# Batch 0 of an attention-and-FFN kernel: mask by a product, single PSUM banks, first weights issued behind the V casts

## The chip, the cores and the metric

The kernel runs on one core of a Trainium2 chip. The metric is the device time of one execution in microseconds (us), lower is better. The median of 7 runs of the kernel before is 380.16 us (379.72 to 381.32).

## The reference

Inputs are `q`, `k`, `v` of shape (8 batches, 8 heads, 576 rows, 64), `s` of shape (8, 8, 576), and the weights `w_gate`, `w_val` (512 x 1536) and `w_out` (1536 x 512), all float32. The attention has a bias that decays with the running sum of `s`, and a causal mask:

```
scores = q @ k.T / 8
cum    = cumsum(max(s, 0))
scores = where(col > row, -1e9, scores + min(-(cum[row] - cum[col]), 0))
attn   = softmax(scores);  x = (attn @ v), heads side by side: 4608 tokens x 512
g = x @ w_gate;  out = (g * sigmoid(g) * (x @ w_val)) @ w_out      # 4608 x 512, float32
```

## The kernel before

**Attention.** A *half batch* is four heads (0 to 3 of a batch, or 4 to 7); there are 16, numbered `hb`. K and Q come in by SyncE's DMA queue (`load_qk`), are cast to bf16 (`cast_half`, `cast_one`), transposed so that the 64 dimensions lie on partitions, and copied into the tile `KQ[hb % 2][r]`, where `r` picks the pair of heads within the half batch. For `hb` up to 4 TensorE does the transposing (`pe_transpose`, `pe_out`), later ones go through DRAM and a transposing DMA (`scratch`, `transposes`, `split`). Besides the 64 dimensions, four more rows of `KQ` hold the running sum of `s` and ones, so that the score product adds the bias by itself; `aug` brings them by small DMAs (`kq<-HL`).

Scores stand transposed: keys on partitions, queries along the free axis. Per head `score_piece` makes four chunks of 512, 512, 512 and 64 columns (`CHUNKS`); chunks 0 and 3 are the blocks on the diagonal, which alone need a mask. ScalarE takes the exponential (L388) into the tile `pt`, GpSimd sets the masked half of the diagonal blocks to zero (`affine_select`, L391 for 512 columns and L396 for 64). `av_piece` multiplies with V, which has a column of ones so that the row sums come along (L413); `av_out` divides on VectorE (L429, L430) into `ot`, two heads side by side. `x_pe` transposes a pair of heads on TensorE into `XT`, the FFN's input (four pairs make the 512 features); later batches do it by DMA (`xs<-ot`, `XT<-xs`).

**FFN.** It goes over nine tiles of 512 tokens (`tt`). Per tile `gate_value` makes 12 gate products (L626) and 12 value products (L641) of 128 x 512, each a sum over four 128-deep parts; ScalarE takes tanh (L631), VectorE multiplies (L633, L649). `down_plain` (tiles 0 and 1, L670) and `down_seven` (L711) multiply with `w_out`.

**Order.** Nothing is scheduled by a planner: each engine works through its instructions in the order in which the program writes them. Batch 0 is written out in `first_batch`. After it, tile `tt` of the FFN is interleaved with attention of batch `tt + 1`: `ffn_items` yields after each product, and `pump` advances `attn_items` up to a position in proportion. `hook` puts a few steps behind the first FFN items, `side` puts loads, casts and copies between the chunks of scores, and `later` holds the copies out of the transposing DMA (`split`, L284), which `do_later` releases one by one.

**PSUM.** There are 8 banks of 512 float32 columns. In batch 0 four of them form two double banks (`wide`), so that a head's scores take two exponentials, of 1024 and 576 columns; the other four serve all else. `second_psum` changes to eight single banks after batch 0. `take` gives the bank that was released first.

**Queues of batch 0.** SyncE's DMA queue has, in this order: `s`, K and Q of half batches 0 and 1, `aug(0)`, V of batch 0, K and Q of half batch 2, `aug(2)`, `aug(3)` (these wait until the scores that read the old rows are done), K and Q of half batch 3, V of batch 1, K and Q of half batches 4 and 5. GpSimd's DMA queue has `aug(1)` and the weights (`w_load`): they are read as float32 and land as bf16, in halves of 768 KB: `g` 0 and `v` 0 behind the scores of head 1, `g` 1 behind head 4, `v` 1 behind head 5, and both halves of `w_out` behind head 7. GpSimd also casts three of the five pieces of V(0), VectorE the other two. In the steady part GpSimd casts V(1) (L183), issues `aug(4)` (L197) and casts K and Q of half batch 4 (L256), in this order.

```
wq = {1: (("g", 0), ("v", 0)), 4: (("g", 1),), 5: (("v", 1),)}
tail = {
    6: ("a0", "a1"),
    7: ("a2", "a3", "a4", "x0", "a5", "x1", "a6", "a7", "x2", "w6", "x3", "w8"),
}
```

Here `a` is a head's values, `x` a pair's transpose and `w` a number of warming products (128-wide products on the identity, whose result nobody reads).

Of the kernel before, what the change touches and what calls it, by code (L numbers as in the profile page):

```python
# [19 lines left out]
def kernel(  # L20
# [86 lines left out]
    PTP = {0: first, "bufs": 8}  # L107

    with tc.manual_schedule():
# [3 lines left out]
        first_psum = ExitStack()  # L113
        psa = first_psum.enter_context(tc.tile_pool(name="psa", bufs=1, space=PSUM))
        bank = {}
        for i in range(2):
            bank["w", i] = psa.tile([128, 1024], FP32, name=f"wide{i}")
        for i in range(4):
            bank["s", i] = psa.tile([128, 512], FP32, name=f"one{i}")
        released = {key: i - 8 for i, key in enumerate(bank)}  # L120
# [3 lines left out]
        def take(kind="s"):  # L124
            b = min((x for x in bank if x[0] == kind), key=lambda x: released[x])
            assert released[b] < OPEN
            released[b] = OPEN
            return b
# [5 lines left out]
        def second_psum():  # L134
            assert all(x < OPEN for x in released.values())
            at_end = dict(released)
            first_psum.close()
            psb = ctx.enter_context(tc.tile_pool(name="psb", bufs=1, space=PSUM))
            bank.clear()
            released.clear()  # L140
            for i in range(8):
                bank["s", i] = psb.tile([128, 512], FP32, name=f"bank{i}")
                released["s", i] = at_end["w", i // 2] if i < 4 else at_end["s", i - 4]

# [6 lines left out]
        def load_one(hb, name, rs=(0, NR)):  # L151
            b, g = divmod(hb, 2)
            if rs[0] == 0:
                loaded[name, hb] = raw.tile([128, NR, J, D], FP32, tag="raw" + name, name="raw" + name)
            nc.sync.dma_start(
                loaded[name, hb][:, rs[0] : rs[1], :, :].rearrange("x r j d -> x r (j d)"),
                SRC[name][0][b, g * HB + 2 * rs[0] : g * HB + 2 * rs[1], :, :].rearrange(
                    "(r e) (p j) d -> (e p) r (j d)", e=2, j=J
                ),
            )  # L160
# [5 lines left out]
        def load_v(b, cs):  # L166
            if 0 in cs:
                loaded["v", b] = raw.tile([128, NCH, H, D], FP32, tag="rawv", bufs=1, name="rawv")
            t = loaded["v", b]
            for c in cs:  # L170
                n = 128 if c < 4 else TAIL
                nc.sync.dma_start(  # L172
                    t[0:n, c, :, :],
                    v[b, :, c * 128 : c * 128 + n, :].rearrange("h p d -> p h d"),
                )
# [10 lines left out]
        NEGS2 = -1.0058441162109375  # L186

# [29 lines left out]
        make_identity(nc, ident)  # L217

# [11 lines left out]
        init_vt(0)  # L230
        init_vt(1)
# [116 lines left out]
        scs = {}  # L348

        def score_piece(bh, ci):  # L350
            hb, hh = divmod(bh, HB)
            pair = bh < H
            if ci == 0:
                pts[bh] = PTP[0].tile(
                [128, PTW], BF16, tag="pt", bufs=PTP["bufs"], name="pt"
            )
# [3 lines left out]
            if pair:  # L360
                if ci % 2 == 0:
                    bs = take("w")
                    scs[bh] = bs
                else:
                    bs = scs[bh]
                base = (512, 0, 0, 512)[ci]
            else:
                bs = take()
                base = 0
            o = base  # L370
            n = sum(hi - lo for _, lo, hi in CHUNKS[ci])
            sc = view(bs, 1024 if pair else 512)
            for (tj, lo, hi) in CHUNKS[ci]:
                w = hi - lo
                nc.tensor.matmul(  # L375
                    sc[:, o : o + w],
                    T[:, 1, e * S + 128 * tj : e * S + 128 * (tj + 1)],
                    T[:, 0, e * S + lo : e * S + hi],
                    start=True,
                    stop=True,  # L380
                )
                o += w
            if not pair or ci % 2 == 1:
                if pair:
                    c0, W = ((576, 1024), (0, 576))[ci // 2]
                else:
                    c0, W = CHUNK_PT[ci], n
                nc.scalar.activation(pt[:, c0 : c0 + W], sc[:, 0:W], AF.Exp, scale=0.125)  # L388
                give(bs)
            if ci == (1 if pair else 0):  # L390
# [90 lines left out]
        def side(h, step, ci):  # L481
# [7 lines left out]
            if NPE <= hb < NHB:  # L489
# [5 lines left out]
                first = 1 if hb < NPE + 2 else 0  # L495
# [31 lines left out]

        def prep_one(hb, i):
# [3 lines left out]
            for r in range(2):  # L532
                pe_out(hb, nm, g, r, nc.scalar if nm == "k" else nc.vector)

        PREP_AT = {
            2: {(0, 3): 0, (1, 3): 1, (2, 1): 2, (2, 3): 3},
# [81 lines left out]

        def gate_value(tt, hps, sus):
            xt = XT[:, :, (tt % 3) * TT : (tt % 3 + 1) * TT]  # L620
            for ft in range(NFT):
                j, f0 = divmod(ft * 128, WCH)
                gbs = take()
                pg = view(gbs, TT)
                for c in range(4):
                    nc.tensor.matmul(  # L626
                        pg, WG[j][:, c, f0 : f0 + 128], xt[:, c, :],
                        start=(c == 0), stop=(c == 3),
                    )
# [8 lines left out]
                vbs = take()  # L638
                pv = view(vbs, TT)
                for c in range(4):  # L640
                    nc.tensor.matmul(  # L641
                        pv, WV[j][:, c, f0 : f0 + 128], xt[:, c, :],
                        start=(c == 0), stop=(c == 3),
                    )
# [209 lines left out]

        cast_half(0, "k", 0, nc.scalar)
# [4 lines left out]
        for nm in ("k", "q"):  # L860
            for g in range(2):
                pe_transpose_half(0, nm, g, 0)
        pe_out(0, "k", 0, 0, nc.scalar)
        pe_out(0, "k", 1, 0, nc.scalar)
        pe_out(0, "q", 0, 0, nc.vector)
        pe_out(0, "q", 1, 0, nc.vector)
# [3 lines left out]
        for nm, eng in (("k", nc.scalar), ("q", nc.vector)):  # L870
            for g in range(2):
                pe_transpose_half(0, nm, g, 1)
                pe_out(0, nm, g, 1, eng)
        cast_one(1, "k", nc.vector)
        cast_one(1, "q", nc.vector)

        def keep_warm(n):
            bs = take()
            for _ in range(n):
                nc.tensor.matmul(  # L880
                    view(bs, 128), ident, ident, start=True, stop=True
                )
            give(bs)

        def first_batch():
            wq = {1: (("g", 0), ("v", 0)), 4: (("g", 1),), 5: (("v", 1),)}
            tail = {
                6: ("a0", "a1"),
                7: ("a2", "a3", "a4", "x0", "a5", "x1", "a6", "a7", "x2", "w6", "x3", "w8"),
            }  # L890
            for h in range(H):
                for ci in range(4):
                    score_piece(h, ci)
                for w in wq.get(h, ()):
                    w_load(*w)
                if h == 1:
                    order = [(nm, g) for g in range(2) for nm in ("k", "q")]
                    for nm, g in order:
                        pe_transpose(1, nm, g)
                    for r in range(2):  # L900
                        for nm, g in order:
                            pe_out(1, nm, g, r, nc.vector)
                    for c in range(3, 5):
                        cast_v(0, c, nc.vector)
                if h == 2:
                    for c in range(3):
                        cast_v(0, c, nc.gpsimd)
                if h == 3:
                    aug(2, SP4)
                if h == 7:  # L910
                    aug(3, SP4)
                    load_qk(3)
                    load_v(1, range(5))
                    load_qk(4)
                    cast_one(2, "k", nc.gpsimd)
                    cast_one(2, "q", nc.gpsimd)
                    load_qk(5)
                    w_load("o", 0)
                    w_load("o", 1)
                for what in tail.get(h, ()):  # L920
                    i = int(what[1:])
                    if what[0] == "a":
                        av_piece(i, range(NCH))
                        av_out(i)
                    elif what[0] == "x":
                        x_pe(i, nc.scalar)
                    else:
                        keep_warm(i)

        first_batch()  # L930
        second_psum()
# [6 lines left out]
        def pump(upto):  # L938
# [13 lines left out]
            4: [lambda: prep_one(2, 3)],  # L952
            6: [lambda: cast_one(3, "k", nc.gpsimd), lambda: cast_one(3, "q", nc.gpsimd)],
        }
        for tt in range(NTT):
# [11 lines left out]
            for i, cost in enumerate(ffn_items(tt)):  # L967
# [3 lines left out]
                if i >= 2 * NFT or i % 4 == 1:  # L971
                    do_later(1)
                for f in hook.pop(n, ()):
                    f()
# [32 lines left out]
```

The softmax here doesn't subtract the row's maximum and nothing guards it: scores larger than these inputs give would overflow.

## Time and profile before

| | |
|---|---|
| median of 7 runs | 380.16 us (379.72 to 381.32) |
| the profiled execution | 380.84 us, its span 379.0 us |
| TensorE matmul busy (PE) | 360.3 us (95%) |
| weight loads (PEld), VectorE (DVE), ScalarE (ACT), GpSimd (POOL) | 229.3, 290.6, 242.4, 206.7 us |
| granted TensorE clock | 1.0 in the page |
| DMA | 64.22 MB, mean 169 GB/s; q1 (SyncE) 46.15 MB, q0 (GpSimd) 17.53 MB |
| first score product, first gate product | 11.29 us, 31.27 us |

A line of the profile's groups names line, engine, operation and tile. "Busy" of PE counts a matmul from its start to a modelled end, 379 ns for 512 columns, though the next one may start 216 ns after it; so a gap of TensorE's work is read from the starts as well as from the listed waits. `SPq` is SyncE's queue: the engine stands at a DMA issue until the queue takes it. Times in a timeline are us from the span's start.

### The profile page before, as it was taken

Reading aid. Unit: us, or ns where it says so; the run is one execution under the profiler, and the core shown is the slowest. Engines: PE = TensorE matmul, PEld = TensorE weight load, DVE = VectorE, ACT = ScalarE, POOL = GpSimd, SP = SyncE. Lnnn points to the kernel's source line nnn. Section 1 sums busy time; section 2 is a strip of 40 time slices with the busy share of each in tenths; the row PEclk is TensorE's granted clock in tenths of the full one; section 3 lists DMA queues with packets and bytes.
Section 4 is the critical chain, followed back from the end, with each engine's and each line's share of the span. In section 5 each row is a group of like instructions: output and inputs, shape, how many; then the busy total and the mean of one; then the engine's idle time right before and its main releaser. Section 6 shows DMA issues by size and latency. Waiting matters only on the chain.

```text
span 379.0 us, 8635 instructions
## 1 busy us (share of the span) xinstructions
PE 360.3 (95%) x3207; PEld 229.3 (61%) x3246; DVE 290.6 (77%) x577; ACT 242.4 (64%) x459; POOL 206.7 (55%) x326
## 2 busy tenths in 40 slices
PE   3789999999999999999999999999999999999996
PEld 3565555655555555965586558755775575466465
DVE  7676776647895899869976999589958876985984
ACT  7686787687986777568767875697365523323321
POOL 7693338455365645595558656775675526224320
PEclk9999999999999999999999999999999999999999
DMA  7899999999478997499769865998233023001103
GB/s 245 186 255 262 199 190 310 319 279 193 159 168 272 214 292 188 120 233 291 159 205 266 219 164 162 226 197 159 48 74 118 20 32 128 0 2 66 45 2 111
DMA packets 100729, 64.22 MB, mean 169 GB/s; under 512 B 81888, under 2 KB 85824, under 8 KB 100688
## 3 DMA queue, kind: packets, MB, share of 16 engines
q1 hardware_dynamic: 91248, 46.15, 49.9%
q0 software_dynamic: 9440, 17.53, 18.7%
q8 instruction: 25, 0.41, 0.5%
q14 instruction: 16, 0.13, 0.1%
HBM read 37.90 MB, written 19.86 MB: 152 GB/s over the span
## 4 chain that ended last, share of the span: by engine, by line
PE 80%; DMA 6%; DVE 4%; SPq 4%; ACT 2%; issue 1%; POOL 1%; DVEq 0%
PE bank L641 20%; PE bank L626 20%; PE bank L711 17%; PE bank L375 8%; PE bank L413 6%; PE bank L670 5%; SPq L172 4%; DMA rawv<-in_v_dram 4%; PE wide L375 2%; ACT pt L388 2%; DMA xs<-ot 1%; DMA kq<-HL 1%; DMA s_sb<-in_s_dram 1%; DVE ht L649 1%; DVE pp L633 1%
## 5 line engine op out<-in xcount | busy, mean ns | idle before, releaser
L388 ACT ACTIVATE pt<-bank 128x512 bf16<-128x512 f32 x224 | 106.8, 506 | 26.1 <-PE bank L375 17.0
L626 PE MATMUL bank<-XT,wg 128*128 128x512 bf16 x420 | 109.7, 379 | 1.2 <-DVE pp L633 0.2
L641 PE MATMUL bank<-XT,wv 128*128 128x512 bf16 x411 | 109.3, 379 | 1.4 <-DMA wv<-in_moe_w_val_dram 0.3
L631 ACT ACTIVATE th<-bank 128x512 bf16<-128x512 f32 x108 | 64.7, 599 | 59.5 <-PE bank L626 55.4
L633 DVE SCALAR_TENSOR_TENSOR pp<-th,bank 128x512 bf16<-128x512 bf16 x108 | 73.7, 682 | 25.9 <-ACT th L631 25.3
L649 DVE SCALAR_TENSOR_TENSOR ht<-pp,bank 128x512 bf16<-128x512 bf16 x108 | 74.1, 686 | 10.5 <-PE bank L641 0.3
L658 POOL TENSOR_TENSOR ht<-ht 128x512 bf16<-128x512 bf16 x35 | 40.5, 1156 | 52.9 <-DVE su L656 52.8
L375 PE MATMUL bank<-kq 128*128 128x128 bf16 (+4 forms) x504 | 67.5, 240 | 0.1
L375 PEld LDWEIGHTS <-kq 128*128 128x128 bf16 x576 | 46.6, 99 | 33.0 <-issue 4.7
L641 PEld LDWEIGHTS <-wv 128*128 128x128 bf16 x432 | 38.3, 98 | 35.8 <-DMA wv<-in_moe_w_val_dram 0.5
L626 PEld LDWEIGHTS <-wg 128*128 128x128 bf16 x432 | 38.4, 98 | 35.3 <-issue 1.3
L391 POOL TENSOR_SCALAR_AFFINE_SELECT pt<-pt 128x512 bf16<-128x512 bf16 x64 | 41.3, 646 | 30.5 <-ACT pt L388 30.0
L413 PEld LDWEIGHTS <-pt 128*128 128x128 bf16 x960 | 41.2, 98 | 17.0 <-issue 1.1
L413 PE MATMUL bank<-vt,pt 128*128 128x65 bf16 x840 | 42.2, 194 | 0.8 <-DVE ot L430 0.5
L447 POOL DMA_DIRECT2D xs<-ot x24 | 21.8, 907 | 28.1 <-DVE ot L430 28.1
L711 PEld LDWEIGHTS <-ht 128*128 128x128 bf16 x336 | 31.2, 98 | 4.3
L197 POOL DMA_DIRECT2D kq<-HL x52 | 32.1, 620 | 0.1
L430 DVE TENSOR_TENSOR ot<-bank,rc 128x320 bf16<-128x320 f32 x56 | 27.5, 491 | 1.9
L396 POOL TENSOR_SCALAR_AFFINE_SELECT pt<-pt 128x64 bf16<-128x64 bf16 x64 | 17.5, 274 | 18.1 <-ACT pt L388 18.0
L711 PEld LDWEIGHTS <-su 128*128 128x128 bf16 x252 | 23.6, 98 | 3.3
L670 PE MATMUL bank<-wo,ht 128*128 128x512 bf16 x90 | 24.2, 379 | 0.3
L776 POOL TENSOR_TENSOR ysb<-ysb 128x512 f32<-128x512 f32 x12 | 15.2, 1270 | 15.3 <-DVE ysb L770 15.3
(96 smaller groups left out, 395.9 us busy)
## 6 DMA issues: line engine op xcount, KB each, us to landing
rawk<-in_k_dram SPq DMA_DIRECT2D x15, 576.0 KB
rawq<-in_q_dram SPq DMA_DIRECT2D x15, 576.0 KB
rawv<-in_v_dram SPq DMA_DIRECT2D x32, 256.0 KB
out_dram<-ysb POOLq DMA_DIRECT2D x32, 256.0 KB, 4.2
xs<-ot POOLq DMA_DIRECT2D x24, 160.0 KB, 3.8
ks<-ck SPq DMA_DIRECT2D x11, 288.0 KB
qs<-cq SPq DMA_DIRECT2D x11, 288.0 KB
wg<-in_moe_w_gate_dram POOLq DMA_DIRECT2D x2, 768.0 KB, 14.0
```

The lines of the kernel that those rows point to most:

```text
L375: nc.tensor.matmul(sc[:, o : o + w], T[:, 1, e * S + 128 * tj : e * S + 128 * (tj + 1)], T[:, 0, e * S + lo : e * S + hi], start=True, sto ...
L388: nc.scalar.activation(pt[:, c0 : c0 + W], sc[:, 0:W], AF.Exp, scale=0.125)
L391: nc.gpsimd.affine_select(pt[:, 1088:1600], pt[:, 1088:1600], pattern=[[0, 4], [1, 128]], compare_op=ALU.is_ge, fill=zreg, base=0, channel ...
L413: nc.tensor.matmul(av[:, bi * (D + 1) : (bi + 1) * (D + 1)], pt[:, c0 : c0 + 128], VT[b % 2][:, tj, h, :], start=(tj == 0), stop=(tj == bi),)
L626: nc.tensor.matmul(pg, WG[j][:, c, f0 : f0 + 128], xt[:, c, :], start=(c == 0), stop=(c == 3),)
L631: nc.scalar.activation(th, pg, AF.Tanh, scale=0.5)
L633: nc.vector.scalar_tensor_tensor(pp, in0=th, scalar=1.0, in1=pg, op0=ALU.add, op1=ALU.mult)
L641: nc.tensor.matmul(pv, WV[j][:, c, f0 : f0 + 128], xt[:, c, :], start=(c == 0), stop=(c == 3),)
L649: nc.vector.scalar_tensor_tensor(hp[:, 2 * k2 : 2 * k2 + 2, :].rearrange("p a n -> p (a n)"), in0=pp, scalar=0.5, in1=pv, op0=ALU.mult, op ...
L658: (nc.vector if ft == NFT - 1 else nc.gpsimd).tensor_sub(hp[:, 1:3, :], hp[:, 1:4:2, :], hp[:, 0:3:2, :])
L670: nc.tensor.matmul(py, hps[ft // 2][:, 2 * (ft % 2) + half, c0 : c0 + 128], WO[ft // WKO][:, ft % WKO, :], start=(ft == 0), stop=(ft == NF ...
L711: nc.tensor.matmul(ps, lhs(p), rhs(p), start=(first and p == 0), stop=(last and p == NP - 1), skip_group_check=True,)
```

## The change

**Batch 0, masks.** A tile `lower` (128 x 512, bf16) holds -32768 above the diagonal of each 128-block and 0 elsewhere. For chunks 0 and 3 a product of the identity with `lower` opens the PSUM bank, and the score products add to it; the exponential makes zeros of the masked places. GpSimd's 16 masks of batch 0 are gone. **Banks.** All eight banks are single from the start; each chunk has its own exponential (three of 512 columns and one of 64 per head). One bank, `spare`, takes the warming products. **Warming.** 32 such products at the very start, and 10 on either side of the second rows' transposes. **Values** follow in twos: heads 0, 1 behind the scores of head 5, 2, 3 behind those of head 6, 4, 5 behind those of head 7, then 6, 7. **Transposes of half batch 1** are split: K behind head 0, Q behind head 1; the copies of the second pair of heads come behind head 3. **Gate products on 3 pairs.** Parts 0 to 2 of gate products 0 and 1 are issued before the FFN begins; part 3 follows in `gate_value`. The last pair's copy into `XT` is on VectorE. **V and weights.** GpSimd casts all five pieces of V(0), and issues the first weights behind them.

```
 # GpSimd's order in batch 0, before
 aug(1); masks of heads 0, 1; w_load g0; w_load v0; masks of head 2; cast_v 0, 1, 2;
 masks of heads 3, 4; w_load g1; masks of head 5; w_load v1; masks of heads 6, 7;
 casts of half batch 2; w_load o0, o1
 # GpSimd's order in batch 0, after
 aug(1); init_vt(0); cast_v 0, 1, 2, 3, 4; w_load g0; w_load v0; w_load g1;
 casts of half batch 2; w_load v1; init_vt(1); w_load o0, o1
```

```diff
 def score_piece(bh, ci):
...
+    masked = bh < H
+    bs = take()
+    n = sum(hi - lo for _, lo, hi in CHUNKS[ci])
+    sc = view(bs, n)
+    masked_here = masked and ci in (0, 3)
+    if masked_here:
+        nc.tensor.matmul(sc, ident, lower[:, 0:n], start=True, stop=False, ...)
...
-                    start=True,
+                    start=not masked_here,
...
+    nc.scalar.activation(pt[:, c0 : c0 + n], sc, AF.Exp, scale=0.125)
+    give(bs)
+    if masked:
+        return
...
+keep_warm(32)
 cast_half(0, "k", 0, nc.scalar)
 cast_half(0, "q", 0, nc.scalar)
 aug(0, SP4)
 load_v(0, range(5))
 load_qk(2)
+row_half("k", 0, nc.scalar)
+row_half("q", 0, nc.vector)
 cast_half(0, "k", 1, nc.scalar)
 cast_half(0, "q", 1, nc.gpsimd)
 aug(1, GP4)
+init_vt(0)
+keep_warm(10)
+row_half("k", 1, nc.scalar)
+row_half("q", 1, nc.vector)
+keep_warm(10)
 cast_one(1, "k", nc.vector)
 cast_one(1, "q", nc.vector)
+for c in range(5):
+    cast_v(0, c, nc.gpsimd)
+w_load("g", 0)
+w_load("v", 0)
+scores(0); half_batch("k"); scores(1); half_batch("q"); scores(2); scores(3)
+for nm in ("k", "q"):
+    for g in range(2):
+        pe_out(1, nm, g, 1, nc.vector)
+aug(2, SP4)
+w_load("g", 1)
+cast_one(2, "k", nc.gpsimd)
+cast_one(2, "q", nc.gpsimd)
+w_load("v", 1)
+scores(4); scores(5); values(0, 1); scores(6); values(2, 3); scores(7)
+aug(3, SP4)
+load_qk(3); load_v(1, range(5)); load_qk(4); load_qk(5)
+init_vt(1)
+values(4, 5); x_pe(0, nc.scalar); values(6, 7)
+x_pe(1, nc.scalar); x_pe(2, nc.scalar); x_pe(3, nc.vector)
+for ft in range(2):
+    products("g", ft, XT[:, :, 0:TT], range(3))
+give(spare)
```

**Smaller moves behind batch 0.** In `prep_one` the copies of the second pair of heads wait until the next FFN item; the first preparation of half batch 3 moves from behind head 8's last chunk to behind head 9's second; the copies (`split`) of half batch 7 begin one head later; `w_load("o", ...)` stands in `hook` at item 5 in the program, which on GpSimd's queue is directly behind `init_vt(1)`.

```diff
-first = 1 if hb < NPE + 2 else 0
+first = 1 if hb < NPE + 3 else 0
...
-2: {(0, 3): 0, (1, 3): 1, (2, 1): 2, (2, 3): 3},
+2: {(1, 1): 0, (1, 3): 1, (2, 1): 2, (2, 3): 3},
...
-    for r in range(2):
-        pe_out(hb, nm, g, r, nc.scalar if nm == "k" else nc.vector)
+    pe_out(hb, nm, g, 0, eng)
+    seconds.append(lambda: pe_out(hb, nm, g, 1, eng))
```

## The prediction

> **What bounds the kernel now.** I read the 40 slices first: TensorE is 90% busy or more from the fourth slice on. So the question is when that stretch begins and what still interrupts it. The waits of TensorE answer the second half, first from 30 to 80 us, then from 62 us to the end.
>
> ```profile
> PE bank L297 <- POOL ck L256: 0.5, 1, 0.5
> PE bank L641 <- DMA wv<-in_moe_w_val_dram: 0.3, 1, 0.3
> PE bank L413 <- POOL vt L183: 0.2, 1, 0.2
> ...
> PE bank L413 <- DVE ot L430: 0.5, 1, 0.5
> ```
>
> After 62 us one wait of 0.5 us is left: the last 317 us are TensorE's own work. Before that, TensorE waits for things that DMAs bring: the first value weights (32.83), V of batch 1 (55.5 and 57.2), and K of heads 16 to 19 (61.6). The chain of waits for 27 to 62 us shows the last two:
>
> ```profile
> 27.59 6.74 SPq L172
> 34.38 7.94 SPq L172
> 42.37 13.58 DMA rawv<-in_v_dram
> 56.00 0.30 POOL vt L183
> 56.56 0.62 POOL vt L183
> 57.92 0.30 POOL kq L197
> 59.70 0.65 POOL pt L391
> 60.53 1.09 POOL ck L256
> 61.67 0.34 PE bank L297 x3
> ```
>
> From 27 to 56 us there is no computing in this chain: the V loads of batch 1 wait behind other transfers, and then GpSimd works through its queue (casts of V, four DMA issues, masks, the cast of K) until TensorE can go on at 61.67. The page's DMA row is at 9 or near it through these slices. So there are two paths to 61.67, TensorE's and this one, and the DMA path is the later. By how much: the stream feeds 0.86 us per four 512-wide products, so the four begun at 60.12 end their feed at 60.98, and the next instruction starts at 61.67: 0.69 lost. The same reading gives 0.43 lost before 57.22 and 0.30 before 55.6. TensorE's own path has 1.4 us to spare.
>
> Next, what the start is paced by. In the timeline of ScalarE each head's scores take one 1024-wide and one 576-wide exponential; the starts 18.21, 19.93, 21.64 give 1.71 us per head, from 12.36 to 26.63. Then masks, values and transposes follow until the first gate product at 31.27. Last, the DMA queues at the weights' issue (15 to 20, 20 to 21 and 22 to 26 us), and the weights' issue itself:
>
> ```profile
> q1 hardware_dynamic: 2427, 1.25, 110.0%
> ...
> q0 software_dynamic: 13, 0.02, 10.9%
> ...
> q0 software_dynamic: 523, 0.78, 108.4%
> ...
> 16.35 0.80 POOL L342 DMA_DIRECT2D wg<-in_moe_w_gate_dram  x1
> 17.14 0.79 POOL L342 DMA_DIRECT2D wv<-in_moe_w_val_dram  x1
> ```
>
> GpSimd issues the first weights at 16.35, but its queue (q0) moves nothing until after 20 us, while SyncE's queue (q1) moves V and the K, Q of heads 8 to 11.
>
> **The change part by part.**
>
> *Start.* 32 + 10 + 10 warming products run while TensorE is idle (it waits 5.4 us for the first cast; the identity is ready by 1.4). The nine scores of the first head take 1.51 us at 11.29 and 0.95 at 17.58, so the clock was half until about 15. The first score still waits for the DMA of 7.93 (landing at 11.24), which the change leaves alone. The exponentials begin after four 128-wide products instead of six up to 448 wide: about 11.7 instead of 12.36, 0.6 earlier.
>
> *Single banks.* Later batches show 512-wide exponentials back to back 0.49 us apart, a 64-wide one 0.11. A head then takes 3 x 0.49 + 0.11 = 1.58 instead of 1.71. With the 0.56 that ScalarE lost between the first two heads, the exponentials end at 11.7 + 8 x 1.58 = 24.3 instead of 26.6. TensorE's part per head is 0.95 plus two mask products, 0.22 and 0.03: 1.2, below 1.58, hidden once the clock is full. If it isn't, a head takes about 1.9 on TensorE and each of the first two costs 0.3.
>
> *Mask by product.* 16 masks leave GpSimd: 8 x 0.647 + 8 x 0.278 = 7.4 us. `lower` adds a fill and a select (about 1 us) before 6 us; GpSimd waited 1.53 at 8.47 for Q, which covers it.
>
> *Values in twos.* After the last exponential come four heads' values (30 products, 1.1 us per two heads), the transposes, and the last pair's normalising (0.7): about 3.1 us instead of 4.6. Gate products could begin at 27.4, and on three pairs they don't wait for the last copy (0.64).
>
> *Weights behind the V casts.* GpSimd casts V as it lands. V's five DMAs are issued from 10.88 to 15.15, and the windows show 2111 packets under 512 B from 15 to 20 us, only 28 of them after 18: the last piece lands before 19, its cast (0.62) ends near 19.6. There the gate weights are issued, 3.2 us later than now; value weights at 20.4; second gate weights at 21.2. Two casts (2.3 us) stand before the second value weights, near 24.4 instead of 23.7; the queue still holds earlier weights then, which covers it. The output weights queue behind all of these in either kernel.
>
> What does this delay cost? Not 3.2 us, if the weights waited for SyncE's queue to drain anyway. q1 is nearly done by 21 (20.8% from 21 to 22 us), and the small DMAs of GpSimd land 2.3 us after issue at 9.14 but 6.5 at 57.31, where q1 is full. I take 0 to 1 us lost on the DMA engines, 0.3 as the value, since work that is not done by one queue is done by the other. The upper bound is the latency of now, 4.2 from issue to the first packets, kept whole: 23.8 instead of about 21.5, 2.3 us lost.
>
> [...]
>
> *K, Q of heads 12 to 15.* Their issue at 26.13 waits for the last score of head 7; with that near 23.5 it comes about 1.7 earlier and halves the weights' share for 1.7 us more: value weights land 0.8 later. So they come at 32.8 + 0.3 + 0.8 = 33.9. TensorE then has only the six products, one more each and five transposes to do, to about 29.8, and idles 4 us. Against now it has three gate products (0.65) behind it: 33.9 - 0.65 - 32.8 = 0.4 late. That lies inside the 1.4 to spare.
>
> [...]
>
> *The 61.67 point.* V of batch 1 lands when all transfers ahead of and beside it are done; their bytes are unchanged and no queue gains. TensorE's order of instructions around that point is unchanged too, so nothing earned before it passes through: the gain of 3.5 us at the gate turns into a wait. The sum is the idle DMA time, +0.3 (0 to 2.3).
>
> *Small moves.* Splitting the preparation's second rows, the copies of batch 7 one step later (0.45 to 1.34 each on VectorE near 110, where TensorE doesn't wait), and the preparation of heads 12 to 15 two pieces later: nothing, as long as VectorE has its idle 2.6 us before 120.3; otherwise half a us.
>
> The profiled execution took 380.84 (span 379.0 and 1.84 around it), 0.68 above the median of the runs. 380.84 + 0.3 - 0.68 = 380.46; I say 380.4.
>
> **The rivals.**
>
> *Slower: the weights come late.* One mechanism: the software queue keeps its 4.2 us from issue to first packet, so from 21.5 to 23.8 the DMA engines idle. Value weights land near 35.9, V of batch 1 2.3 us later, and 61.67 becomes 64. [...] Against: all slow first packets in the trace stand beside a full q1. It decides from 0.8 us of idle DMA time on. Price +2.3: 382.5. [...]
>
> *Faster: V of batch 1 comes earlier.* One DMA engine ends each weight transfer later than the others, and V's third and fourth pieces wait for it. If the shifted queues even this out, or the earlier issue of K, Q lets V through before the weights end, the chain to 61.67 shortens by up to the 1.4 that TensorE has to spare: 379.0. Against: the bytes are the same.
>
> *No effect of the start: the exponentials do not end earlier*, because TensorE is cold or the K rows are late. Then the gate begins near 30, still before the value weights: 380.4 again. That is my forecast's own number.
>
> **How the numbers follow.** A measurement of this kernel can tell about 0.2%, 0.76 us, from no change. My forecast (idle DMA time below 0.8, with the no-effect case) has 0.43; the slower rival with all its smaller forms 0.37; the faster one 0.20. The range reaches from a little beyond the faster rival's price, 378.8, to the slower's, 382.5. The likeliest case's own range is 379.4 to 380.9.
>
> **What the next profile would show.** Right: exponentials ending near 24.3, gate products near 27.7, a TensorE wait for wv of 3 to 4 us, q0 moving from 21 to 22 us, and again a wait for the cast of K near 61.7. Wrong: first q0 packets after 23; an instruction rate at half after 30 us; V of batch 1 cast before 54.5 or after 57; or no wait near 61.7, which would mean that TensorE's path is the later one.

## The result and the profile after

| | before | after |
|---|---|---|
| median | 380.14 us (47 runs) | 382.02 us (19 runs, 381.15 to 383.63) |
| ratio, 95% interval | | 1.0051 [1.0039, 1.0064] |
| profiled execution | 380.84 us, span 379.0 | 381.85 us, span 380.1 |

The changed kernel is slower by 1.9 us, well beyond the 0.2% that a measurement can tell. The time lies inside the range on record, but the likeliest case ("no change", 379.4 to 380.9) did not come; the slower rival, weights that come late, did, and it is its price of 382.5 that takes the result into the range.

All listed waits of TensorE between 20 and 80 us, in the profile after (total, times, longest):

```profile
PE bank L615 <- DMA wv<-in_moe_w_val_dram: 4.0, 1, 4.0
PE bank L615 <- DMA wg<-in_moe_w_gate_dram: 0.3, 1, 0.3
PE bank L615 <- DVE pp L631: 0.3, 1, 0.3
PE bank L445 <- DVE ot L412: 0.2, 1, 0.2
```

The wait for the value weights has grown from 0.3 us to 4.0. The timeline of TensorE shows what surrounds it (start, duration, what, and in brackets the idle time before it):

```profile
28.24 1.69 PE L615 MATMUL bank<-XT,wg 128*128 128x512 bf16 x6 [0.29 <-DMA wg<-in_moe_w_gate_dram]
...
34.19 1.89 PE L615 MATMUL bank<-XT,wv 128*128 128x512 bf16 x4 [3.99 <-DMA wv<-in_moe_w_val_dram]
```

Gate products begin at 28.24 instead of 31.27, so the start did get faster. Then TensorE stands, and the first four value products take 1.89 us where the same four took 1.04 before. The reason is in a table by stretches of 3.41 us, cut at 33.66 and 37.07, where the granted clock changes, and 3.41 ahead of them (stretch, length, busy time of PE, PEld, DVE, ACT, POOL with counts, then granted clock, DMA share, GB/s):

```profile
30.25:33.66 3.41, 0.00 (x0) 0.00 (x0) 0.69 (x1) 1.68 (x3) 0.72 (x1) 1.00 1.12 285
33.66:37.07 3.41, 2.88 (x13) 1.49 (x14) 0.95 (x2) 0.00 (x0) 0.43 (x1) 0.50 1.13 243
```

TensorE did nothing in the first stretch, and its clock was half in the whole of the second. Last, the chain of waits:

```profile
20.97 13.18 DMA wv<-in_moe_w_val_dram
34.19 1.89 PE bank L615 x4
...
59.23 1.16 POOL kq L183 x2
60.41 0.65 POOL pt L373
61.24 1.09 POOL ck L245
62.38 0.45 PE bank L286 x5
```

Here are both holds in one chain: 13 us on the value weights from their issue, and again the cast of K in front of the transposes, at 62.38 instead of 61.67. From that point on the two profiles run 0.7 apart; the last 0.4 of the 1.1 in span is at the ending. Because the profiled execution of before was 0.7 above its median, the pair shows only 1.0 of the 1.9 us.

Where did the weights lose their time? They were issued here, 3.8 us later than before:

```profile
20.18 0.80 POOL L331 DMA_DIRECT2D wg<-in_moe_w_gate_dram  x1
20.97 0.79 POOL L331 DMA_DIRECT2D wv<-in_moe_w_val_dram  x1
```

SyncE's queue q1 ran dry between 21 and 22 us (0.38 MB from 20 to 21, 0.02 from 22 to 23), and GpSimd's queue q0 was hardly moving yet. The DMA queues between 22 and 23 us:

```profile
DMA packets 50, 0.07 MB, mean 72 GB/s; under 512 B 5, under 2 KB 44, under 8 KB 50
...
q0 software_dynamic: 35, 0.05, 85.5%
q1 hardware_dynamic: 15, 0.02, 8.4%
```

The share (85.5%) says that packets are open; the bytes (0.05 MB) say that little arrives. In a usual execution of before (run e5 below) the same microsecond carries this:

```profile
DMA packets 145, 0.22 MB, mean 218 GB/s; under 512 B 9, under 2 KB 144, under 8 KB 144
...
q0 software_dynamic: 119, 0.18, 100.2%
```

From 21 to 24 us it is 0.41 MB after and 0.67 MB in e5. The missing 0.26 MB are 1.2 us at the 215 to 225 GB/s of those stretches. The runs' profiles fall into two groups: 0.61 to 0.69 MB where the weights are issued between 15.6 and 16.6 us (before, e4, e5, e7, e11, e12), 0.36 to 0.45 where it is after 19 (after, e2, e3, e6, e8, e10). In e1 (0.61) and e9 (0.85) the weights were issued earlier still, ahead of K and Q of heads 8 to 11, so that other transfers fill these microseconds.

### The profile page after: what moved, and what is told of

It reads as the page before. It is cut to its first block, busy times and chain, and to the rows that moved or that the text cites. A ratio compares the mean times of both kernels' runs of the same rounds, so it can differ in the third digit from the quotient of the medians.

```text
span 380.1 us, 8752 instructions
## 1 busy us (share of the span) xinstructions
PE 364.0 (96%) x3260; PEld 232.0 (61%) x3300; DVE 289.7 (76%) x576; ACT 242.7 (64%) x474; POOL 202.9 (53%) x314
## 4 chain that ended last, share of the span: by engine, by line
PE 83%; DMA 6%; DVE 4%; SPq 2%; issue 1%; POOL 1%; ACT 1%; DVEq 0%; ACTq 0%; POOLq 0%
PE bank L615 44%; PE bank L704 17%; PE bank L358 9%; PE bank L395 7%; PE bank L663 5%; DMA wv<-in_moe_w_val_dram 3%; DMA rawq<-in_q_dram 1%; DMA rawv<-in_v_dram 1%; DVE pp L631 1%; SPq L157 1%; DVE ht L642 1%; PE bank L286 1%; DVE wo L600 1%; DVE kq L273 0%; DVE ot L412 0%
## 5 line engine op out<-in xcount | busy, mean ns | idle before, releaser
L368 ACT ACTIVATE pt<-bank 128x512 bf16<-128x512 f32 (+1 forms) x256 | 120.2, 509 | 28.4 <-PE bank L358 19.8
L358 PE MATMUL bank<-kq 128*128 128x128 bf16 (+4 forms) x576 | 75.1, 240 | 0.3
L358 PEld LDWEIGHTS <-kq 128*128 128x128 bf16 x576 | 45.7, 98 | 29.7 <-issue 1.3
L373 POOL TENSOR_SCALAR_AFFINE_SELECT pt<-pt 128x512 bf16<-128x512 bf16 x56 | 36.2, 646 | 29.2 <-ACT pt L368 28.7
L395 PEld LDWEIGHTS <-pt 128*128 128x128 bf16 x960 | 41.1, 98 | 16.6 <-issue 0.7
L395 PE MATMUL bank<-vt,pt 128*128 128x65 bf16 x960 | 46.1, 194 | 0.5 <-DVE ot L412 0.5
L412 DVE TENSOR_TENSOR ot<-bank,rc 128x320 bf16<-128x320 f32 x64 | 31.4, 491 | 2.2
L378 POOL TENSOR_SCALAR_AFFINE_SELECT pt<-pt 128x64 bf16<-128x64 bf16 x56 | 15.1, 270 | 20.4 <-ACT pt L368 20.2
```

Source lines behind the costliest of these rows:

```text
L358: nc.tensor.matmul(sc[:, o : o + w], T[:, 1, e * S + 128 * tj : e * S + 128 * (tj + 1)], T[:, 0, e * S + lo : e * S + hi], start=not maske ...
L368: nc.scalar.activation(pt[:, c0 : c0 + n], sc, AF.Exp, scale=0.125)
L373: nc.gpsimd.affine_select(pt[:, 1088:1600], pt[:, 1088:1600], pattern=[[0, 4], [1, 128]], compare_op=ALU.is_ge, fill=zreg, base=0, channel ...
L395: nc.tensor.matmul(av[:, bi * (D + 1) : (bi + 1) * (D + 1)], pt[:, c0 : c0 + 128], VT[b % 2][:, tj, h, :], start=(tj == 0), stop=(tj == bi),)
```

## The experiments

My theory after the first look: late issue leaves the DMA engines partly idle, everything behind it (value weights, V of batch 1, K of heads 16 to 19) comes that much later, and TensorE has no spare for it. The rivals: the half clock alone, the extra matmuls on TensorE, the earlier K, Q of heads 12 to 15. Line numbers of kernels with added lines move by one or two.

**Weights first (e1).** The changed kernel, with the first weights in front of the V casts:

```diff
         aug(1, GP4)
+        w_load("g", 0)
+        w_load("v", 0)
         init_vt(0)
...
             cast_v(0, c, nc.gpsimd)
-        w_load("g", 0)
-        w_load("v", 0)
```

> The changed kernel, but GpSimd issues the first gate and value weights directly behind aug(1), near 12.3 us, ahead of filling and casting V. Theory 'late weights' (the delay of the first weights costs the time, through the DMA path to the cast of K at 61): the weights flow from 20.6 at the latest, wg lands at 27.7 or earlier, the idle DMA time at 21 to 23 us is gone, the cast of K ends at 61.6 as in the kernel before, and the time is 380.0 to 380.4. If the two queues share the DMA engines from 13 us on, wv lands before 30, the 4 us wait of TensorE and the half clock behind it are gone too, and V of batch 0 comes later. Rival 'batch 0 itself' (masks by product, single banks, the reordered start cost the time): 381.7 to 382.3, unchanged.

Measured 385.72 us, ratio 1.0155 [1.0136, 1.0173]: the worst of all; neither of the expected times came. Issued at 12 us, the weights flow beside q1, though not at once: of q0's bytes in the next rows 0.12 MB come between 15 and 16 us, 3 us after the issue. The queues from 12 to 16 us:

```profile
q1 hardware_dynamic: 2614, 0.66, 74.7%
q0 software_dynamic: 145, 0.14, 23.8%
```

The gate weights landed at 21.36, but V of batch 0 shared the engines with them, and its casts ended at 27.84 instead of 20.23:

```profile
PE bank L395 <- POOL vt L168: 6.6, 3, 3.2
```

TensorE's clock was half, too, from 22.89 to 33.13, in and behind these waits. So neither end of the order is free: too early holds up V (6.6 us of waits here), too late leaves the engines partly idle (0.41 MB for 0.67 from 21 to 24 us, above).

**Filling the idle time (e2).** The changed kernel with 64 warming products in front of the first value product (`fill(n)` issues n products of the identity with itself into a bank of its own):

```diff
-            1: [lambda: prep_one(2, 0)],
+            1: [lambda: prep_one(2, 0), lambda: fill(64)],
```

> The changed kernel, with 64 warming products (3.6 us) put between the first preparation of half batch 2 and the first value product, in the stretch in which TensorE idles from 30.2 to 34.2 us. Rival 'clock' (the half clock from 33.7 to 37.1 makes TensorE's path the later one): the clock stays at 1.0, the four value products take 0.86 instead of 1.89 us, and the time falls by 1 to 1.9 to 380.1 to 381.0. Theory 'late weights': the clock stays at 1.0 and TensorE gains 1.5 us at 37, but it waits for the cast of K at 61 to 62 all the same; 381.6 to 382.0.

Measured 381.36, ratio 1.0036 [1.0019, 1.0052]. That lies between the two expectations. The clock stayed full (mean 0.999 in the profile), and about 0.6 us of the 1.9 came back, with overlapping intervals. In the profile waits for V and the cast of K stand in the place of the half clock:

```profile
PE bank L395 <- POOL vt L168: 1.1, 2, 0.8
PE bank L286 <- POOL ck L245: 0.5, 1, 0.5
```

The profile itself gains nothing: the cast of K ends at 62.30, in the profile after at 62.32, and the spans are both 380.1. Three executions of the changed kernel had a mean clock of 0.999 or 1.0; they took 381.73, 381.88 and 382.08 us, close to the median of 382.02. So the half clock is at most the smaller part of the loss, and that it is a part is not shown.

**Only the late weights (e3).** The kernel before, with the first weights moved behind GpSimd's three casts of V (issue at 19.95); nothing else of the change:

```diff
-            wq = {1: (("g", 0), ("v", 0)), 4: (("g", 1),), 5: (("v", 1),)}
+            wq = {4: (("g", 1),), 5: (("v", 1),)}
...
                         cast_v(0, c, nc.gpsimd)
+                    w_load("g", 0)
+                    w_load("v", 0)
```

> The kernel before, with one part of the change alone: the first gate and value weights are issued behind GpSimd's three casts of V, near 20.4 us instead of 16.35. Theory 'late weights': wg lands at 28.2 or later, wv 0.7 to 1.5 later than 32.8, the cast of K ends near 62.3, and the time is 381 to 382. Rival 'batch 0 itself': 380.2, no change.

Measured 381.65, ratio 1.0048 [1.0027, 1.0070]. This one move costs what the whole change costs, within the intervals, without the mask products and without the earlier K, Q of heads 12 to 15. Its queues from 21 to 24 us carry 0.36 MB, again against 0.67:

```profile
DMA packets 269, 0.36 MB, mean 121 GB/s; under 512 B 27, under 2 KB 263, under 8 KB 269
```

and TensorE waits where the prediction had seen spare time:

```profile
PE bank L413 <- POOL vt L183: 0.8, 2, 0.5
PE bank L297 <- POOL ck L256: 0.5, 1, 0.5
```

**Is there 1.4 us to spare? (e4, e5).** e4 is the kernel before with 18 more warming products on TensorE just before the first gate product, 1.05 us, as 64 such products take 3.74 us in e2; e5 is the kernel before again, for one more profile.

```diff
-                7: ("a2", "a3", "a4", "x0", "a5", "x1", "a6", "a7", "x2", "w6", "x3", "w8"),
+                7: ("a2", "a3", "a4", "x0", "a5", "x1", "a6", "a7", "x2", "w6", "x3", "w26"),
```

> The kernel before with 18 more warming products (1.0 us of TensorE) directly ahead of the first gate product. If TensorE's path has 1.4 us to spare against the DMA path at 61.67, as the prediction says, the gate begins 1 us later, the wait for the cast of K shrinks from 0.7 to about 0, and the time stays within 0.3 of 380.1. If TensorE's path decides: 381.1.

> The kernel before, unchanged, for a second profile of it. The profile that the prediction read took 380.84, 0.7 above the median, and the cast of K at 61.62 ended last there; with 18 more warming products it ended at 60.03 and TensorE did not wait for it. Theory 'two paths, nearly even' (which of them ends last changes from one execution to the next): here the cast of K ends anywhere from 60.0 to 61.7, and where it ends by 60.5 TensorE has no wait of over 0.3 us from 50 to 62 us, and the time is 379.3 to 380.1. Rival (the DMA path is always the later one): the cast ends at 61.4 to 61.8, with the same waits as in the profile shown.

e4: 380.92, ratio 1.0033 [1.0021, 1.0045]: 1.0 us in, about 1.25 out (0.8 to 1.7), no spare. e5: 380.07, close to the median of before. Its waits of TensorE from 27 to 66 us, all of them:

```profile
PE bank L626 <- DVE pp L633: 0.2, 1, 0.2
PE bank L375 <- DVE ht L649: 0.2, 1, 0.2
PE one L463 <- DVE ot L430: 0.2, 1, 0.2
PE bank L626 <- ACT XT L468: 0.2, 1, 0.2
```

No weights, no V, no cast of K: the three waits from which the prediction read its 1.4 us are not there. In e5 the value weights land at 30.38 (e4: 29.66), in the profile that I had read at 32.83, with the same issue order; there one of the 16 engines ended each weight transfer late (gate weights 27.68, the one before it 26.39; value weights 32.83 and 30.69). The cast of K, in e5 and then in the profile after:

```profile
59.20 1.14 POOL L256 CAST ck<-rawk 128x1152 bf16<-128x1152 f32 x1
61.18 1.14 POOL L245 CAST ck<-rawk 128x1152 bf16<-128x1152 f32 x1
```

It ends 2.0 us later in the changed kernel, and the span is 1.9 us longer (378.2 and 380.1). Against this usual execution the whole loss is there at 62 us, on the DMA path; the pair of the first profiles showed 0.7 of it.

**K, Q of heads 12 to 15 (e6).** The changed kernel, with these loads on GpSimd's queue behind the first value weights:

```diff
         w_load("v", 0)
+        load_one(3, "k", eng=nc.gpsimd)
+        load_one(3, "q", eng=nc.gpsimd)
...
-        load_qk(3)
```

> The changed kernel, with K and Q of half batch 3 issued by GpSimd behind the first value weights instead of by SyncE at 24.8 us, so that they don't share the DMA engines with these weights. [...] V of batch 1 starts earlier beside the weights, but all bytes ahead of the cast of K are the same: it ends at 62.3 as before. 'TensorE's path decides in the changed kernel': 379.6 to 380.4. 'The DMA path decides': 381.2 to 382.0.

Measured 382.29, ratio 1.0067 [1.0043, 1.0091]; no gain. In its profile the value weights land at 31.24 and the wait for them shrinks from 4.0 us to 1.8, with a mean clock of 0.999, but TensorE now waits 2.9 for V of batch 1:

```profile
PE bank L395 <- POOL vt L168: 2.9, 3, 1.8
PE bank L615 <- DMA wv<-in_moe_w_val_dram: 1.8, 1, 1.8
PE bank L286 <- POOL ck L245: 0.5, 1, 0.5
```

The bytes are the same; moving them between queues exchanged one wait for another. The lower of the expected ranges, 379.6 to 380.4, has TensorE's path gain 1.6 to 2.4 us, and no run shows such a gain: behind waits for the value weights of 2.5 and 2.6 us the clock was half in e12 and full in e8, and their medians are 381.12 and 381.64.

**Weights behind two casts (e7).** The changed kernel, with the first weights behind the second of the five casts of V (16.25 us):

```diff
-        for c in range(5):
+        for c in range(2):
             cast_v(0, c, nc.gpsimd)
         w_load("g", 0)
         w_load("v", 0)
+        for c in range(2, 5):
+            cast_v(0, c, nc.gpsimd)
```

> The changed kernel, with the first gate and value weights issued behind the second cast of V (near 16.6 us) instead of the fifth (20.2). At that time three of the five pieces of V have passed, so V is not held up as in the first experiment, where issue at 12 us cost TensorE 6.6 us of waiting for V. Theory 'the software queue's start costs DMA time': it starts before SyncE's queue has run dry, the weights land 0.5 to 1.3 us earlier than in the changed kernel (wv 32.9 to 33.6), the cast of K ends by 61.7, and the time falls by 0.7 to 1.9, to 380.1 to 381.3. [...]

Measured 381.05, ratio 1.0031 [1.0013, 1.0049]: about 0.8 us of the 1.9 back, inside the range on record. From 21 to 24 us the engines now move 0.64 MB:

```profile
DMA packets 444, 0.64 MB, mean 215 GB/s; under 512 B 17, under 2 KB 444, under 8 KB 444
```

The value weights land at 30.30, the casts of V of batch 1 end at 55.38 instead of 57.88, and still V decides. That profile, 379.84, is 1.2 us below the kernel's own median, and reads well for it:

```profile
PE bank L395 <- POOL vt L168: 1.5, 3, 0.9
...
PE bank L615 <- DMA wv<-in_moe_w_val_dram: 0.5, 1, 0.5
PE bank L286 <- POOL ck L245: 0.5, 1, 0.5
```

**Half of the output weights later (e8).** The changed kernel, with the second output weights behind the casts of V of batch 1:

```diff
             for c in range(5):
                 cast_v(1, c, nc.gpsimd)
+            w_load("o", 1)
...
-            5: [lambda: w_load("o", 0), lambda: w_load("o", 1)],
+            5: [lambda: w_load("o", 0)],
```

> The changed kernel, with the second half of the output weights issued behind GpSimd's casts of V of batch 1 instead of near 27 us. The queue ahead of V of batch 1 is 5 us shorter, so its last pieces land near 52 instead of 56 and the cast of K ends by 60; the DMA path is out of the way at 61.7. What is left is TensorE's own path, with its idle stretch and half clock. 'The DMA path decides in the changed kernel': 380.0 to 380.8. 'TensorE's path decides': 381.6 to 382.0, unchanged. If the second half of the output weights comes too late (after 63.5), TensorE waits in the first down product and the time is over 382.5.

Measured 381.64, ratio 1.0037 [1.0015, 1.0059]. That is the second theory's figure, TensorE's path. V no longer makes TensorE wait; the output weights do:

```profile
PE bank L616 <- DMA wv<-in_moe_w_val_dram: 2.6, 1, 2.6
PE bank L664 <- DMA wo<-in_moe_w_out_dram: 1.7, 1, 1.7
```

**Taking the later DMA hold away (e9, e10, e11).** To see what is left without the hold at 62 us, three kernels leave out the load of the second output weights, so that V of batch 1 lands earlier (in e8, where that load stands behind the casts of V, they end at 53.60, in the profile after at 57.88): the kernel before (e9), the changed kernel (e10), and the changed kernel with e7's order (e11). The edit of e9; in the other two the load is taken out of `hook`:

```diff
-    WO = [const.tile([128, WKO, DM], BF16, name=f"wo{j}") for j in range(NFT // WKO)]
+    WO = [const.tile([128, WKO, DM], BF16, name="wo0")] * (NFT // WKO)
...
-                    w_load("o", 1)
```

> The kernel before, with the second half of the output weights left out (one DMA, about 5 us of all DMA engines; both halves of the down products read the first half, so the output differs). V of batch 1 then lands some 5 us earlier and the DMA path is far below TensorE's. Theory A (in a usual execution of the kernel before TensorE's and VectorE's own path already decides; the 1.4 us to spare belonged to one execution): 379.0 to 379.6, 0 to 1 us below the median of before, with no wait for V or the cast of K. Theory B (TensorE has 1.4 us to spare, as the prediction read it): 378.5 or less.

> The changed kernel, with the second half of the output weights left out in the same way. Theory A (V of batch 1 and the wait for the value weights hold the changed kernel back): V no longer waits, the 4 us wait for the value weights stays, about 380, that is about 2 below the changed kernel's 382.0 and near the kernel before. Theory B (the loss lies on TensorE: half clock, more matmuls): 381.5 or more.

> The changed kernel with the first weights issued behind the second cast of V, and the second half of the output weights left out. Both DMA holds are then small. Theory A (the change does take about 3 us off TensorE's path, which the DMA path hides): 376.5 to 378, some 2 to 3 below the kernel before without that half. Theory B (the start gains nothing that lasts): within 0.7 of the kernel before without that half.

| | median | ratio to before | value weights land, in the profile |
|---|---|---|---|
| e9 | 379.82 | 0.9983 [0.9966, 1.0000] | 31.09 |
| e10 | 382.44 | 1.0050 [1.0028, 1.0072] | 33.49 |
| e11 | 379.21 | 0.9970 [0.9948, 0.9991] | 31.55 |

In all three profiles no wait for V or the cast of K is left between 27 and 66 us. e9: the DMA path holds the kernel before by 0.65 us in the median (0 to 1.3), not by 1.4; the time is just above the first theory's 379.0 to 379.6. Its profile, 378.44, is a short execution: the clock was full from 8.88 us on, in the profile of before from 14.99, and the gate products began at 29.10. e10 was a miss for my theory: I expected 380, since I took V for the larger hold, and the median did not move at all. What is left in e10 is the first hold alone, the wait for the value weights with the half clock behind it (a mean of 0.62 from 33.4 to 37.5 us), and it is enough: e10 is 2.6 us above e9 in the medians and 2.7 in the profiles.

```profile
PE bank L615 <- DMA wv<-in_moe_w_val_dram: 3.5, 1, 3.5
PE bank L615 <- DMA wg<-in_moe_w_gate_dram: 0.3, 1, 0.3
```

Of its 12 executions the only one with a mean clock of 1.0 took 379.14 us; the others, at 0.989 to 0.996, took 380.66 to 384.04. One execution is little, but here, with the hold at 62 us out of the way, there is no later hold for the half clock to vanish in.

So in the changed kernel two holds stand one behind the other, at 34 and at 62 us, and each covers the other: the second taken away gives nothing (e10), the first eased gives 0.8 (e7), both give 2.8 (382.02 to 379.21, e11), of which the kernel before gains 0.65 without that load, too (e9). e11 was a miss on the other side, too: I expected 376.5 to 378, two to three us below e9, and it came 0.6 below it, with overlapping intervals. Its profile shows what is left:

```profile
PE bank L615 <- DMA wv<-in_moe_w_val_dram: 2.1, 1, 2.1
PE bank L615 <- DVE pp L631: 0.3, 1, 0.3
```

TensorE is ready for the value products at 29.5 and gets the weights at 31.6; in e9 it is ready later and gets them at 31.1. The faster start ends in this wait even when everything else is out of its way.

**A version that might beat both (e12).** The full computation: e7's order, and the second output weights behind the first cast of V of batch 1.

```diff
             for c in range(5):
                 cast_v(1, c, nc.gpsimd)
+                if c == 0:
+                    w_load("o", 1)
...
-            5: [lambda: w_load("o", 0), lambda: w_load("o", 1)],
+            5: [lambda: w_load("o", 0)],
```

> Full computation: the changed kernel with the first weights issued behind the second cast of V, and the second half of the output weights issued behind the first cast of V of batch 1. V of batch 1 lands some 5 us earlier (casts end near 51), the second half of the output weights is issued near 48 and lands near 59 to 61. Theory A (two paths, the later decides): 377.5 to 379.0, faster than both kernels by about 1 and 3 us, with a wait for the output weights of 0 to 1.5 us left. Theory B (the start gains nothing that lasts): 379.5 or more.

Measured 381.12, ratio 1.0028 [1.0008, 1.0047]: no better than e7, and slower than the kernel before; the second theory's side. The second output weights and V come in time; the wait for the value weights stays, 2.5 us in its profile, and with it the half clock (0.50 from 32.89 to 36.30). I found no order that beats the kernel before.

## Why the prediction's likeliest case was wrong, and where it was right

*Right, with the sizes.* The V casts, the issue behind them, the gate products on time, the idle stretch and the landing of the value weights came as worked out: 20.2 for the last cast's end (19.6 predicted), gate products at 28.24 (27.7), the wait 4.0 (4), the landing 34.15 (33.9). The extra for K, Q of heads 12 to 15 held in part: they were issued 1.3 us earlier (1.7 predicted), and between the first of the 16 engines' ends of gate and of value weights lie 4.4 us in e2, e8 and e10 and 3.75 in e4 and e5, so 0.7 for a predicted 0.8. In e3, which leaves K, Q where they were, it is 3.94, and 5.5 in the profile after. That the weights' share falls beside these loads stands in the profile of before: q0 moved 0.62 MB in the 3 us from 26, and 0.84 in the 7 us from 29, beside 1.06 on q1. The step "nothing earned before it passes through" was right, with one correction: what takes the start's gain is first the value weights' landing, and only then the 61.67 point.

*Right, but too slow.* Exponentials ended at 25.37, not 24.3: they began at 11.40, and a head took 1.75 us instead of 1.58. TensorE's waits for exponentials before the mask products, 0.9 in all, are in the profile; how the rest comes about was not tried. It cost nothing, since TensorE then waited 0.3 for the gate weights and 4.0 for the value weights.

*The first failed step: "I take 0 to 1 us lost on the DMA engines, 0.3 as the value".* Measured by missing bytes it is 1.2 us here and 1.4 in e3. That lies between the prediction's point of decision (0.8) and its bound (2.3); I put the value below both. The reasoning that failed was "work that is not done by one queue is done by the other": that needs the second queue to be ready when the first runs dry, and q0, issued at 20.18, moved 0.01 MB in the microsecond from 21, 0.05 from 22 and 0.16 from 23. The prediction's own sign for being wrong, "first q0 packets after 23", was drawn too crudely: nine packets come between 21 and 22, and the rate comes two microseconds later. Two other signs did come: half the instruction rate after 30 us (granted clock 0.50 from 33.66 to 37.07), and V of batch 1 cast after 57 (57.88).

*When the weights flow.* In the profile of before q0 moved nothing from 15 to 20 us, and the prediction took from it that the weights may have waited for SyncE's queue to drain. e1 and e9 show them flowing beside q1. In e1, issued at 12 us, weights and V flow together from 15 us on (0.14 MB on q0, 0.66 on q1 from 12 to 16). In e9 the weights were issued at 14.33, when q1 was as full as at the issue in before (0.22 MB in that microsecond in both). But K and Q of heads 8 to 11 were issued behind them (14.97 and 15.63), in before ahead of them (15.20 and 15.91, the weights 16.35). The queues of e9 from 17 to 18 us:

```profile
q0 software_dynamic: 75, 0.12, 82.7%
q1 hardware_dynamic: 318, 0.08, 47.7%
```

From 21 to 22 us both still flow, 0.11 and 0.17 MB. So the row in the profile of before did not show that a full q1 keeps q0 waiting: the weights flowed behind K and Q where they were issued behind them, and ahead where they were issued ahead. What makes this order was not tried. Nor does it give the loss, which lies in the time from issue to the first full rate.

*The second failed step: "TensorE's own path has 1.4 us to spare".* The three gaps were real in that execution, which was 0.7 us above the median. e4 and e5 show no spare in usual executions, and e9 shows 0.65 us (0 to 1.3) in the median. With the DMA term at 0.3 this did little harm to the number. But the forecast has no time for the half clock behind the idle stretch, and that costs 1.3 at the place (the second tanh comes 2.93 us after the value weights land, 1.62 in e11, where the clock was full), and e2 gets about 0.6 of it back in the median, with overlapping intervals.

*The sum, made again:* 380.14 + 1.2 for idle DMA time = 381.3, for 382.02 measured; 0.7 stays open. The 0.6 of e2 would fill it, but two paths that meet at 62 us don't add up: in the profile after the cast of K ends last there, with or without the half clock. Between e5 and the profile after the DMA path alone is 2.0 us later, of which the missing bytes explain 1.2; the rest was not traced, and the spread of the 16 engines' ends (below) is larger.

*The rivals.* "The weights come late" was the mechanism, with 1.5 us from issue to the first packets and 2.8 to the rate instead of 4.2 to the first packets, and 1.9 in all instead of 2.3. Of "V of batch 1 comes earlier" nothing was seen; V's casts ended 0.7 later (2.0 later than in e5). "No effect of the start" did not happen: the start was 3 us faster, and it was the transfers that did not follow.

## What to carry to other kernels

When a prefetch is moved later, ask what the DMA engines do between the end of the work that is queued and the first full rate of the work that is issued late, and count bytes per microsecond there; a high share of open packets can hide idle time (85.5% beside 0.05 MB in the microsecond from 22). Spare time read from one execution is a property of that execution (1.4 us in the one that the prediction read, none in e4 and e5): where two paths end within a microsecond of each other, take a second profile, or add a known amount of work to one path, before an edit is costed at nothing. And a faster stage in front of a transfer earned here only up to the transfer's landing (gate products 3.0 us earlier, then a wait of 4.0); where two such holds stand one behind the other, taking one away proves little about the other (nothing in e10, 2.8 us for both in e11).

## What the runs showed of the hardware

*A half clock behind 0.90 us of work.* In the profile after the half clock lasts 3.413 us (33.66 to 37.07), in e1 three times as long (22.89 to 33.13); the full clock lasts 375.47 us in e8, 110 times as long. The records of the full clock begin at 6.35 us in the profile after and at 4.35 in e8, whose program is the same there. A step below is a stretch of 3.41 us, counted in each run from where its records begin. In the profile after the half step follows one without any work of TensorE. In e12 it follows one with 0.90 us of matmul (in e1 one with 0.98 us, from 19.48 to 22.89):

```profile
29.48:32.89 3.41, 0.90 (x9) 0.44 (x7) 0.69 (x1) 1.98 (x3) 0.00 (x0) 1.00 1.11 277
32.89:36.30 3.41, 3.41 (x17) 1.87 (x15) 2.42 (x4) 1.64 (x3) 1.14 (x1) 0.50 1.11 266
```

In e8 TensorE waited as long, 2.6 us, but the wait, from 29.87 to 32.46, lies across two steps with 1.57 and 2.61 us of work, and the clock stayed full:

```profile
28.24:31.65 3.41, 1.57 (x11) 0.76 (x9) 0.92 (x2) 1.97 (x3) 0.00 (x0) 1.00 1.11 267
31.65:35.07 3.42, 2.61 (x21) 1.55 (x22) 1.53 (x3) 1.04 (x2) 0.36 (x1) 1.00 1.11 279
```

So a wait of 2.5 us came with a half step in one execution and one of 2.6 with none in another.

*About 3 us from issue to rate in these runs.* Issued at 19.4 to 20.2 us (after, e2, e3, e6, e8, e10), the gate weights' first engine ends 6.5 to 6.7 us after the issue. With 3.75 us for the transfer alone (the step from the first engine's end of the gate weights to that of the value weights in e4 and e5) that gives an estimate of 2.8 to 2.9 us from issue to full rate, though q1 is nearly empty by then (0.02 MB from 22 to 23 us in the profile after). With q1 busy it took no longer: in e1 and e9, issued at 12.0 and 14.3, q0 first moves over 0.1 MB in a microsecond from 15 to 16 and from 17 to 18. Issued between 15.65 and 16.5, behind K and Q (before, e4, e5, e7, e11, e12), the first engine ends at 24.6 to 24.8 whatever the issue. These flow at full rate from about 21, when q1 runs dry (q0 moves 0.17 MB from 21 to 22 us in before and 0.16 in e5, q1 0.07 and 0.09), and their 3 us are over by then.

*The last of the 16 engines.* From the first engine's end of the gate weights to the last one's it is 0.5 to 3.0 us in these profiles (2.96 in the one that the prediction read, 1.23 in e4, which issues them alike). For the value weights the first ends stand at 28.42 and 28.39 in these two, the last at 32.83 and 29.66. The first value product starts behind the last one (32.88 in the profile of before), so this alone moved the landing by 3.2 us from one execution to another.
